# Two taps of the shifted k in one VectorE product, and dy written over the gradient's rows

## The chip, the cores and the metric

One core of a Trainium2 chip. The metric is device time in microseconds (us). The profile follows one execution; its times are from the start of that execution's span. PE is the matmul engine (PEld its weight loads), DVE the vector engine, ACT the scalar engine, POOL GpSimd, and SP the engine that issues most of the DMAs. Every engine works through its own instructions in a fixed order and waits at semaphores for the others.

## The reference, cut to what matters

The kernel computes a layer's output and its gradients. With S = 2048 positions, D = 512 channels:

```
xn      = layernorm(q)
k_shift = sum over t = 0..3 of k[s - t] * shift_k[:, t]        # per channel, bf16
kv      = k_shift * v
y       = causal long convolution of kv with ssm_k (by FFT)  + kv * ssm_D
out     = q + xn * y + (xn W_gate * xn W_up) W_down
gradients of out with respect to q, k, v, shift_k, ssm_k, ssm_D, W_gate, W_up, W_down
```

The gradient that enters is `grad_out` (go). The convolution's backward pass starts from dy = go * xn, which must go through the same transform as kv and as ssm_k.

## The kernel before, in words

Position s = 16 p + r lies on partition p, row r. The rows are handled as eight blocks b of two rows, so that a block of q, k, v or go is a tile of 128 x 2 x 512 bf16 (256 KB). There are three stretches.

*The front* (to about 120 us). The DVE normalizes each block (`norm`, L315 to L345: statistics, a root on ACT at L331, a reciprocal, the rows, then a store of xn to `XN` in DRAM). `kernel_spec` (L407) turns ssm_k around and sends its sixteen rows through the first transform matmul, `stage1` (L360); the results in PSUM are evicted to `fst` by DVE and ACT in turn, and `wgu_transposes` (L442) turns the two up-projections around. `pre(b)` (L376) makes for a block dy = go * xn (L381), the four-tap sum `ks` from `kh` (L389, L391, L392), stores `ks` to `KS` in DRAM (L397), multiplies it by v (L399), and sends dy and kv through `stage1`. `kh` is k with three boundary rows ahead of its sixteen; it is loaded by four DMAs (`load_k`, L308): rows 0 to 2 by two, rows 3 to 10 and rows 11 to 18 by one each. `skb` holds the taps on all partitions.

*The feed-forward part.* `ffn1(ch)` and `yb(ch)` (L495, L537) run the gated layer for chunks ch of 256 positions. They fill `hd`, which is stored to `HDD` in DRAM, and `bx`, which is stored to `BX`. Work of the front and of the spectral groups (`groups`, L737) is the side generator, and the loop at L883 takes some steps of it after each step of the main one.

*The rest* (from about 300 us): inverse transforms, weight gradients, and the final elementwise work. The change does not touch it.

What sets the order: each call emits instructions, and a scheduler then places them on each engine's queue; up to the end of `tables(3)` (L699) the program fixes the relative order of those engines' instructions by `manual_schedule`, but a later instruction whose inputs are there can still be put between them. The tile framework adds the waits. It also takes care of memory: the pool `st1` (L675) is laid over that of the tables' temporaries and can be written only when those are done. In `st1` lie `kh`, `dy_b`, `t_b` and the turned ssm_k tiles `kn`, one buffer each of `dy_b` and `t_b`. The tiles of q and go (`x_b`, `go_b`, L298 and L304) lie in another pool, with four and three buffers. So the load of block b + 4 of q, and of block b + 3 of go, must wait until the earlier block's last reader is done. PSUM tiles of two banks (`pf`, `pgu`, `ptk`, `pw`) share three buffers (L252), so a matmul group waits for the eviction of the group three before it. SP issues loads and stores in one queue. Each DMA signals one of eight semaphores in turn, so an issue also waits for the landing of the DMA eight issues before it.

Of the kernel before, what the change touches and what calls it, by code (L numbers as in the profile page):

```python
# [8 lines left out]
BF = mybir.dt.bfloat16  # L9
F32 = mybir.dt.float32  # L10
I32 = mybir.dt.int32
ALU = mybir.AluOpType
# [6 lines left out]
D = 512  # L19
F = 1376  # L20
R = 16
P = 128
# [168 lines left out]
def kernel(  # L191
# [24 lines left out]
    nc = tc.nc  # L216
# [45 lines left out]
    skb = const.tile([P, 4, D], BF, name="skb")  # L262
# [97 lines left out]
    def stage1(sig, src, i, r, evac):  # L360

        if r % 2 == 0:
            FST[sig] = stp.tile([P, 2, 2, D], BF, name="fst", bufs=4)
        st = FST[sig]
        pf = P2("pf", [P, 2, D])
        for c in range(2):
            point = sig == 0 and r == 0
            nc.tensor.matmul(pf[:, c, :], lhsT=TB.W1[:, c, :], rhs=src[:, i, :], start=True, stop=not point)  # L368
            if point:

                nc.tensor.matmul(pf[:, c, :], lhsT=TB.W1[0:1, c, :], rhs=Drow, start=False, stop=True)
        evac(st[:, :, r % 2, :], pf[:])
        if r % 2 == 1:
            nc.sync.dma_start(FD[sig, :, :, r - 1:r + 1, :], st[:])

    def pre(b):  # L376

        xn, go = XG.pop(b)
        v = VB.pop(b)
        dy = ST["st1"].tile([P, 2, D], BF, name="dy_b")  # L380
        nc.vector.tensor_tensor(dy[:], go[:], xn[:], op=ALU.mult)  # L381
        yield
        ks = stp.tile([P, 2, D], BF, name="ks_b")
        t = ST["st1"].tile([P, 2, D], BF, name="t_b")
        for n, j in enumerate((3, 2, 1, 0)):
            src = ST["kh"][:, 2 * b + 3 - j:2 * b + 5 - j, :]
            w = skb[:, j:j + 1, :].to_broadcast((P, 2, D))
            if n == 0:
                nc.vector.tensor_tensor(ks[:], src, w, op=ALU.mult)  # L389
            else:  # L390
                nc.vector.tensor_tensor(t[:], src, w, op=ALU.mult)  # L391
                nc.vector.tensor_tensor(ks[:], ks[:], t[:], op=ALU.add)  # L392
            if n == 1:
                stage1(2, dy, 0, 2 * b, act)
                stage1(2, dy, 1, 2 * b + 1, act)
                yield
        nc.sync.dma_start(KS[:, 2 * b:2 * b + 2, :], ks[:])  # L397
        kv = v
        nc.vector.tensor_tensor(kv[:], ks[:], v[:], op=ALU.mult)  # L399
        yield  # L400

        def last():
            stage1(1, kv, 0, 2 * b, act)
            stage1(1, kv, 1, 2 * b + 1, act)
        LATE.append(last)
# [265 lines left out]
    ST = {}  # L671
# [40 lines left out]
    def front():  # L712
        for b in range(8):
            if b == 0:
                late_loads()
                with tc.issue_after(TB.last.ins):
                    norm(2)
            elif b < 6:
                norm(b + 2)
            if LATE:  # L720
                LATE.pop(0)()
            yield
            if b == 0:
                yield from kernel_spec()
                yield from wgu_transposes()
                WTS.append(True)
            if 0 < b < 7:
                load_v(b + 1)
            yield from pre(b)
            if b < 5:  # L730
                load_x(b + 3)
        LATE.pop(0)()
        yield
# [470 lines left out]
```

## Time and profile before

| | us |
|---|---|
| median of 3 runs | 488.27 |
| all runs | 490.54, 488.27, 486.96 |
| the profiled execution | 485.82 |
| its span, first to last instruction | 484.1 |
| PE busy in the span | 470.3 |
| DVE busy | 340.6 |
| ACT busy | 318.2 |
| DVE, the 24 products L391 | 16.5 |
| DVE, the 24 additions L392 | 16.5 |
| DVE, the 8 products L389 | 5.5 |
| DVE, the 8 products L381 | 5.4 |

The profiled execution took 485.82 us, 1.7 more than its span. Durations are of single instructions; consecutive DVE instructions overlap by some 0.07 to 0.09 us, so an instruction of 0.69 us holds the queue for about 0.60.

### The profile page before, as it was taken

To read this page: it belongs to the slowest core of one execution; us is meant where nothing else is said; L and a number is where in the kernel's file an instruction comes from. 1 tells how busy PE (TensorE), PEld (TensorE's weight loads), DVE (VectorE), ACT (ScalarE), POOL (GpSimd) and SP (SyncE) were. 2 spreads that over 40 slices of the span, in tenths; PEclk is the share of its full clock that TensorE was granted. 3 is DMA by queue.
4 is the path that set the end of the run, shared out by engine and by line. 5 is a ranking of instruction groups with operands and counts; after the bars stand their busy time and mean duration, and the time that the engine had idled before them with its cause. 6 is when DMAs were issued, how large, how long until landed. Compare 5 with 4: busy or idle time off the path is not lost.

```text
span 484.1 us, 10517 instructions
## 1 busy us (share of the span) xinstructions
PE 470.3 (97%) x4335; PEld 313.7 (65%) x4335; DVE 340.6 (70%) x622; ACT 318.2 (66%) x354; POOL 15.3 (3%) x31
## 2 busy tenths in 40 slices
PE   7998999999999999999999999999999999999977
PEld 6866754647638547447447744567777788777775
DVE  7889969988274768667686865013276899999780
ACT  4976896759658678779779974466577524543141
POOL 8010000000000000000000000020000000000000
PEclk9999999999999999999999999999999999999999
DMA  8999998999997965978968298999999979699747
GB/s 269 374 379 359 294 263 313 349 308 338 310 303 277 252 220 196 295 251 254 301 214 258 78 334 294 399 327 307 321 396 384 367 263 404 203 254 245 209 149 246
DMA packets 105469, 139.87 MB, mean 289 GB/s; under 512 B 33323, under 2 KB 78800, under 8 KB 103758
## 3 DMA queue, kind: packets, MB, share of 16 engines
q1 hardware_dynamic: 103838, 137.84, 86.1%
q10 hardware_dynamic: 1584, 1.36, 1.0%
q8 instruction: 34, 0.56, 0.5%
q14 instruction: 13, 0.11, 0.1%
HBM read 68.45 MB, written 63.41 MB: 272 GB/s over the span
## 4 chain that ended last, share of the span: by engine, by line
PE 61%; DVE 21%; DMA 13%; issue 2%; ACT 2%; SPq 0%; DVEq 0%; ACTq 0%
PE px L553 16%; PE pgu L510 13%; PE py L546 8%; PE pdh L516 6%; PE pu L1038 5%; DMA out_dram<-o 4%; PE pf L368 3%; PE pg L611 3%; PE ps L582 3%; PE pd L1002 2%; DMA HDD<-hd 2%; DVE dxn L1126 2%; DVE tk L1093 2%; DVE dxn L1120 2%; DVE e L1121 2%
## 5 line engine op out<-in xcount | busy, mean ns | idle before, releaser
L553 PE MATMUL px<-WT,hd 128*128 128x512 bf16 (+1 forms) x352 | 81.0, 380 | 0.0
L1038 PEld LDWEIGHTS <-xnC 128*128 128x128 bf16 x704 | 67.1, 98 | 8.8 <-issue 0.9
L553 PEld LDWEIGHTS <-hd 128*128 128x128 bf16 (+1 forms) x352 | 32.8, 98 | 44.4 <-issue 7.5
L1038 PE MATMUL pu<-natd,xnC 128*128 128x256 bf16 x512 | 58.5, 273 | 0.2 <-ACT nath L235 0.2
L235 ACT CAST GO<-pg 128x1024 bf16<-128x1024 f32 x48 | 46.3, 1017 | 12.8 <-PE pg L611 6.6
L235 ACT CAST SP<-ps 128x1024 bf16<-128x1024 f32 x48 | 46.6, 1029 | 11.9 <-PE ps L582 10.9
L510 PE MATMUL pgu<-xt,Wu 128*128 128x256 bf16 (+1 forms) x352 | 53.2, 273 | 0.6 <-DVE fst L238 0.4
L235 ACT CAST gu<-pgu 128x1024 bf16<-128x1024 f32 (+1 forms) x48 | 45.4, 947 | 12.3 <-PE pgu L510 11.9
L510 PE MATMUL pgu<-xt,Wg 128*128 128x256 bf16 (+1 forms) x352 | 52.8, 273 | 0.2 <-DMA Wg<-in_B_w_gate_dram 0.2
L598 DVE TENSOR_TENSOR T<-SP 128x2048 bf16<-128x2048 bf16 x24 | 29.4, 1223 | 30.8 <-ACT SP L235 30.8
L516 PE MATMUL pdh<-gt,WdT 128*128 128x256 bf16 (+1 forms) x352 | 47.1, 273 | 0.1
L510 PEld LDWEIGHTS <-Wu 128*128 128x128 bf16 (+1 forms) x352 | 32.9, 100 | 14.7 <-issue 10.2
L546 PE MATMUL py<-Wd,hd 128*128 128x512 bf16 (+1 forms) x176 | 41.4, 380 | 0.0
L235 ACT CAST og<-pu 128x1024 bf16<-128x1024 f32 (+1 forms) x11 | 10.9, 994 | 46.2 <-PE pu L1038 25.6
L235 ACT CAST fst<-pf 128x1024 bf16<-128x1024 f32 x40 | 39.1, 1034 | 0.8 <-ACT dh L235 0.5
L235 ACT COPY natd<-pt 128x2048 bf16<-128x2048 bf16 x16 | 30.0, 1876 | 13.5 <-PE pt L846 13.5
L516 PEld LDWEIGHTS <-WdT 128*128 128x128 bf16 (+1 forms) x352 | 34.9, 100 | 5.2 <-issue 0.2
L510 PEld LDWEIGHTS <-Wg 128*128 128x128 bf16 (+1 forms) x352 | 34.8, 100 | 4.1 <-DMA Wg<-in_B_w_gate_dram 0.5
L530 DVE TENSOR_TENSOR hd<-gu 128x512 bf16<-128x512 bf16 (+1 forms) x48 | 19.1, 398 | 19.0 <-ACT gu L235 19.0
L531 DVE TENSOR_TENSOR hd<-gu,dh 128x1024 bf16<-128x1024 bf16 (+1 forms) x48 | 30.8, 642 | 1.0
L1002 PE MATMUL pd<-goC,nath 128*128 128x512 bf16 x128 | 30.1, 379 | 0.0
L546 PEld LDWEIGHTS <-hd 128*128 128x128 bf16 (+1 forms) x176 | 16.4, 98 | 20.7 <-issue 3.3
(171 smaller groups left out, 698.0 us busy)
## 6 DMA issues: line engine op xcount, KB each, us to landing
HDD<-hd SPq DMA_DIRECT2D x35, 384.0 KB, 3.6
FD<-fst SPq DMA_DIRECT2D x24, 512.0 KB, 4.5
X<-FD SPq DMA_DIRECT2D x24, 512.0 KB, 4.7
GD<-GO SPq DMA_DIRECT2D x24, 512.0 KB, 3.9
g<-GD SPq DMA_DIRECT2D x12, 1024.0 KB, 7.9
hb<-HDD SPq DMA_DIRECT2D x8, 1344.0 KB, 8.5
bb<-BX SPq DMA_DIRECT2D x8, 512.0 KB, 6.9
BX<-bx SPq DMA_DIRECT2D x7, 512.0 KB, 3.6
```

The source lines that it names most:

```text
L235: nc.scalar.copy(o, i)
L368: nc.tensor.matmul(pf[:, c, :], lhsT=TB.W1[:, c, :], rhs=src[:, i, :], start=True, stop=not point)
L510: nc.tensor.matmul(pgu[:w, i, t, :], lhsT=W[:, c, f0:f0 + w], rhs=xt[:, :, c, :], start=(c == 0), stop=(c == NC4 - 1))
L516: nc.tensor.matmul(pdh[:w, i, :], lhsT=WdT[:, c, f0:f0 + w], rhs=gt[:, :, c, :], start=(c == 0), stop=(c == NC4 - 1))
L530: nc.vector.tensor_tensor(hd[:fw, fb0:fb0 + n, 0, :], gu[:fw, :n, 0, :], gu[:fw, :n, 1, :], op=ALU.mult)
L531: nc.vector.tensor_tensor(hd[:fw, fb0:fb0 + n, 1:3, :], gu[:fw, :n], dh[:fw, :n].unsqueeze(2).to_broadcast((fw, n, 2, 256)), op=ALU.mult)
L546: nc.tensor.matmul(py[:], lhsT=hd[:fw, fb, 0, ss], rhs=Wd[:fw, fb, :], start=(fb == 0), stop=(fb == NFB - 1))
L553: nc.tensor.matmul(px[:], lhsT=hd[:fw, fb, t, ss], rhs=W[:fw, fb, :], start=(t == 1 and fb == 0), stop=(t == 2 and fb == NFB - 1))
L582: nc.tensor.matmul(ps[32 * q:32 * q + 32, a, :], lhsT=TB.EF[64 * a:64 * a + 64, 4 * g + q, ri].rearrange("p k j -> p (k j)"), rhs=X[64 * a ...
L598: tt(W[:].rearrange("p c a d -> p c (a d)"), A[:, i:i + 1].rearrange("p c a d -> p c (a d)").to_broadcast((P, 2, 2 * D)), B[:].rearrange(" ...
L1002: nc.tensor.matmul(pd[:fw, :], lhsT=nat_h(fb, r), rhs=goC[:, r, :], start=(r == 0), stop=(r == R - 1))
L1038: nc.tensor.matmul(pu[:, c, :, :fw], lhsT=xnC[:, r, cs(c)], rhs=nat_d(fb, r), start=(r == 0), stop=(r == R - 1))
```

## The change

Two edits in `pre(b)`. dy no longer has a tile of its own: it is written over the block's go tile. And the four taps are taken two at a time: one product of 128 x 2048 elements (two taps, two rows, 512 channels) reads three rows of `kh`, the middle one twice, and the taps' rows in falling order; its result `t` has twice the size. Each pair of taps is then added up in `ks`. So a block has two products and three additions in place of four products and three additions.

```
-        dy = ST["st1"].tile([P, 2, D], BF, name="dy_b")
+        dy = go
         nc.vector.tensor_tensor(dy[:], go[:], xn[:], op=ALU.mult)
         yield
         ks = stp.tile([P, 2, D], BF, name="ks_b")
-        t = ST["st1"].tile([P, 2, D], BF, name="t_b")
-        for n, j in enumerate((3, 2, 1, 0)):
-            src = ST["kh"][:, 2 * b + 3 - j:2 * b + 5 - j, :]
-            w = skb[:, j:j + 1, :].to_broadcast((P, 2, D))
-            if n == 0:
-                nc.vector.tensor_tensor(ks[:], src, w, op=ALU.mult)
+        t = ST["st1"].tile([P, 2, 2, D], BF, name="t_b")
+        for n in (0, 2):
+            s = ST["kh"][:, 2 * b + n:2 * b + n + 3, :]
+            part, row, elem = s.ap
+            src = bass.AP(s.tensor, s.offset, [part, [row[0], 2], [row[0], 2], elem])
+            w = skb[:, 2 - n:4 - n, :]
+            part, row, elem = w.ap
+            w = bass.AP(w.tensor, w.offset + row[0], [part, [-row[0], 2], [0, 2], elem])
+            nc.vector.tensor_tensor(t[:], src, w, op=ALU.mult)
+            nc.vector.tensor_tensor(ks[:], t[:, 0] if n == 0 else ks[:], t[:, 0 if n else 1], op=ALU.add)
+            if n:
+                nc.vector.tensor_tensor(ks[:], ks[:], t[:, 1], op=ALU.add)
             else:
-                nc.vector.tensor_tensor(t[:], src, w, op=ALU.mult)
-                nc.vector.tensor_tensor(ks[:], ks[:], t[:], op=ALU.add)
-            if n == 1:
                 stage1(2, dy, 0, 2 * b, act)
                 stage1(2, dy, 1, 2 * b + 1, act)
                 yield
```

In the additions, the pair n = 0 writes `ks = t[0] + t[1]`; the pair n = 2 adds `t[0]` and then `t[1]`.

Nothing else in the source differs. The scheduler puts the changed program's instructions in another order, though, on DVE, ACT and SP, between the start and some 120 us; on PE six matmuls (three `pdh`) come earlier and the rest keeps its order, and POOL's order is the same. After 130 us all the orders agree. The lines behind L397 have numbers larger by 3 in the changed kernel.

## The prediction

> **What bounds the kernel now.** I read the page first, then busy time by stretches, then the waits, then the queues one by one.
>
> ```profile
> PE 470.3 (97%) x4335; PEld 313.7 (65%) x4335; DVE 340.6 (70%) x622; ACT 318.2 (66%) x354; POOL 15.3 (3%) x31
> PE   7998999999999999999999999999999999999977
> DVE  7889969988274768667686865013276899999780
> ```
>
> PE is nearly full everywhere, so a change in the front is worth what it adds to or takes from PE's waits there. The table by stretches (PE, PEld, DVE, ACT, POOL, then clock, DMA share, GB/s) and the waits of PE up to 170 us show where these are:
>
> ```profile
> 24.00:36.00 12.00, 11.31 (x98) 8.14 (x96) 10.74 (x24) 8.80 (x12) 1.37 (x1) 1.00 1.07 382
> 36.00:48.00 12.00, 10.18 (x87) 7.73 (x86) 11.20 (x20) 8.45 (x10) 0.00 (x0) 1.00 0.96 362
> 48.00:60.00 12.00, 11.60 (x107) 8.82 (x105) 11.90 (x20) 9.98 (x13) 0.00 (x0) 1.00 0.91 288
> ...
> PE ptk L413 <- DVE fst L238: 1.5, 1, 1.5
> ...
> PE pf L368 <- ACT fst L235: 0.9, 1, 0.9
> ```
>
> From 36 to 60 us the DVE has no idle time left, and PE waits for its evictions (fst): 1.48 at 41.97, and again at 57.87. The 0.9 is at 77.99. From 84 to 120 PE shows no wait. The DVE, in turn, starts that stretch by waiting for k, and k waits its turn on SP. DVE's timeline, then SP's:
>
> ```profile
> 32.30 1.18 DVE L238 CAST fst<-pf 128x1024 bf16<-128x1024 f32 x1
> ...
> 36.76 0.69 DVE L389 TENSOR_TENSOR ks_b<-kh,skb 128x1024 bf16<-128x1024 bf16 x1 [1.99 <-DMA kh<-in_A_k_dram]
> ...
> 40.70 1.22 DVE L238 CAST fst<-pf 128x1024 bf16<-128x1024 f32 x1
> ```
>
> ```profile
> 25.45 1.56 SPq L348 DMA_DIRECT2D XN<-x_b  x2
> 27.06 0.45 SPq L300 DMA_DIRECT2D x_b<-in_A_q_dram  x1
> 27.77 1.20 SPq L534 DMA_DIRECT2D HDD<-hd  x2
> 29.57 0.34 SPq L310 DMA_DIRECT2D kh<-in_A_k_dram  x1
> 30.42 0.37 SPq L311 DMA_DIRECT2D kh<-in_A_k_dram  x1
> ```
>
> The reader sees k's boundary rows issued at 29.57 and 30.42 and used at 36.76, while the DMA share is about 1: transfers land in turn, some 6.3 us after their issue.
>
> **The change part by part.** *Cheaper products.* The groups by form give the price:
>
> ```profile
> L598 DVE TENSOR_TENSOR T<-SP 128x2048 bf16<-128x2048 bf16 x24 | 29.4, 1223 | 30.8 <-ACT SP L235 30.8
> L391 DVE TENSOR_TENSOR t_b<-kh,skb 128x1024 bf16<-128x1024 bf16 x24 | 16.5, 686 | 0.2
> ```
>
> Two products of 0.687 become one of 1.22: 0.15 saved, 16 times, 2.4 us of DVE by 118 us. Four such pairs lie in the full stretch 36 to 60 (0.6 us); the others lie where PE does not wait for the DVE. L391 and L598 each read a row of one operand twice and still add 1024 elements for 0.53 us. No row of the trace reads an operand's rows in falling order. Its bounds are 1.22 and about 2.3 us (with float32 operands 256 elements take 0.42 in L1067 and 512 take 0.69 in L548, 1.04 ns an element, so 2048 take 2.3); I take 1.22, from the row of the same shape and type. The Trainium skill ("VectorE: DVE Perf Modes", What auto-detection actually checks) asks of the faster mode that tensors be 16-bit with step one along the elements, which by that rule leaves 1.22 standing; no run so far shows a falling row.
>
> *dy without st1.* dy's tile no longer waits for the tables' memory, so the order puts dy(0) right behind the first rows, ahead of the copy of xt at 8.44 (idle 0.49 before it), and dy(1) between the masks at 22.75 and 22.93. The first costs 0.1, which the 0.64 us of idle time at 12.72 covers. The second pushes what follows on DVE by 0.60; it takes 0.60 out at 31.09, where dy(0) stood.
>
> *SP, the step that costs most.* With dy(0) and dy(1) done early, two loads of q, blocks 4 and 5, come free and are put on SP ahead of k: XN(0), XN(1), x3, **x4**, HDD, **x5**, HDD, k. But x4 goes into block 0's buffer, which the store XN(0) still reads. That store is issued at 25.45 and lands 6.3 later, at 31.8. So SP, which stood free at 27.5, stands until 31.8; behind it wait two HDD stores, x5 (XN(1) lands at 32.4) and all of k. At 0.5 us each (35.19 to 35.72 in SP's timeline), k's boundary rows are issued at 33.8 and 34.3 in place of 29.57 and 30.42. When do they land? From below: 34.3 plus 3.1, the landing time of the FD store at 57.88, is 37.4. From above, in turn: x4 at 31.8 + 3.2 (v at 79.1) = 35.0, HDD 1.0, x5 0.66, HDD 1.0 (spacings of the landings at 32.4 to 35.1), k 1.65 (35.1 to 36.76): 39.3. I take K = 38.8, nearer the upper end because DMA share is 1 there: 2.0 later.
>
> *DVE and ACT behind it.* In the new order the statistics of x3 stand ahead of the first fst; x3 lands at 33.1 (27.06 + 6.0), so that fst runs at 35.4, not 32.30. PE's second group of stage one and the ACT wait for it, but k is later still. Then ACT has the root of x3 ahead of the eviction of gu(1), and that root needs an aggregate that the DVE makes only behind the first wide product. Counted from K: product 1.15, aggregates 0.25, root 0.2, gu 1.0: at K + 2.6 PE gets its buffer; pf 0.43, pdh 0.22; the next pgu needs the second fst, at K + 3.25 (1.15 + 0.2 + 0.62 + 0.1 + 1.15), and takes 1.75, pdh 0.22, pf 0.43: the transposes that waited at 41.97 start at K + 5.75. Before it was 36.76 + 5.21. So PE is later by 2.0 + 0.54 = 2.6 at this point. The rest of the stretch up to the fst at 56.60, summed the same way (four products at 1.15, seven more operations at 0.60 to 0.65, two more statistics at 0.60, the same evictions), ends 21.75 behind K, before 21.06: 2.6 or 2.7 again, with 0.7 us of slack at each PE wait between. The 0.6 us of cheaper products are in this sum; the two statistics, drawn forward because x4 is there early, eat them.
>
> *58 to 84.* The evictions of the turned weights on ACT (59.45) and PE behind them shift as they are. A new wait: go(3) now reuses the tile that PE's dy(0) matmuls read until 68.5, before only DVE's dy. So go(3) is issued at 71.2 (before 61.73), lands 3.4 later (go at 70.07), and DVE stands at dy(3) for it, with the aggregate of x6 behind: dy 0.6, reciprocals 0.25, sum 0.6, rows 1.3, product 1.15, aggregates 0.2; ACT's root waits for that with fst of dy(1) behind it, 1.3: PE at 77.55 plus the shift. Before, PE stood at 77.99. So 0.45 is won back: 2.15 is left. v's load, also freed by PE, was so before. The root of x7 comes next: from 78.8 the DVE has two wide products, ten operations of 0.6 and two statistics up to x7's aggregate, about 9.4, so root and gu(2) end on ACT at 89.5; PE wants that buffer at 87.31 + 2.15 = 89.5: nothing more, and nothing to spare. Later dy and kv are made 2 to 9 us before PE takes them, and go(4) to go(7), issued when PE's dy three blocks before is done, land over 10 us before theirs is due.
>
> **Sum.** 2.0 (k later) + 0.54 (order) - 0.45 (won back) = +2.1 us. The profiled execution is 485.82 (span 484.1 and 1.7 around it), so 487.9; it lies 2.4 under the median of the runs shown, 488.27, and against that the forecast is 490.4.
>
> **The rivals.** *Hidden:* k is not late. If the engines are empty enough for K = 37.4 or less, or if the loads land as before, +0.5 to +1.1 is left of the order and 0.45 to 0.9 comes back at 77.99: +0.2, 488.5. For it: SP's pause empties the DMA queue. Against: five transfers of 1.66 MB then come in a bunch.
>
> *Faster:* every saved 0.15 counts, because DVE is full from 36 to 60 and 9 to 10 tenths until 118: -2.4 us, 485.9. It decides if K stays at 36.8 and PE's wait at 77.99 (0.9) goes. Against it: beyond 84 us PE has no wait. The Trainium skill ("VectorE: DVE Perf Modes", Rules for kernel authors) says to minimize the count of DVE operations; by that rule the 16 fewer would show.
>
> *The go ring:* go(3) or go(4) lands after 6.3 us, as in the crowd at 25, not 3.4. Then ACT's root at 79 is 2.9 later and PE stands for it: 493.3. For it: three blocks of go now hang on PE, and SP stands at each.
>
> *Falling rows at half speed:* 16 x 1.1 us more DVE. Four lie in the full stretch: 4.3, less 0.7 slack; the other twelve overrun the idle DVE of 60 to 118 by about 3: +9 in all, 497.5.
>
> **How the numbers follow.** Forecast 0.58, hidden 0.17, faster 0.08, go ring 0.11, half speed 0.06. The range: K from 37.4 to 39.3 and an error of 1 us in the sums give +0.2 to +3.8, so 488.5 to 492.1; the three runs shown lie 3.6 apart, half of which I add on both sides: 486.7 to 493.9. That reaches the go ring and most of the hidden case, and leaves out half speed and most of the faster one. A measurement tells about 1% from no change, 4.9 us. Faster by over 1%: 0.03, a third of the faster case; slower: all of half speed, half of the go ring, a little of the forecast: 0.14; within 1%: 0.83.
>
> **What would show it.** Right: SP's k issues at 33.5 to 34.5 with x4 at 31.8 ahead; the first wide product at 38 to 39.5 with DVE idle before it; wide products of 1.22 us; the transposes L413 (now L416) at 44 to 45; DVE waiting for go(3) near 74. Wrong: k's product at 37 or before, or products of 2 us, or PE waits between 84 and 120, or another time in the rest, which I take as unchanged.

## The result, and the profile after

The changed kernel took 493.46 us (median of six runs, 491.06 to 494.09); the kernel before, run beside it, 487.72 (six runs). The ratio is 1.0101, with a 95% interval of 1.0068 to 1.0134. The profiled execution took 494.09, with a span of 491.9.

Where the time went is read by setting each matmul of the one trace against the same matmul of the other. PE's order is nearly the same, so the difference of the start times is how far PE is behind at that point:

| before, us | changed is later by |
|---|---|
| to 29 | 0.0 |
| 31.8 | 1.15 |
| 34.4 | 0.55 |
| 35.3 to 36.1 | 1.18 |
| 42.0 (the transposes L413) | 6.19 |
| 44 to 56 | 6.20 |
| 58 to 76 | 5.94 |
| 84 to 382 | 5.86 |
| 394 to 459 | 10.19 |
| 471 to the end | 7.85 |

Nearly all of the change's own loss arises between 36 and 42 us. It stays at 5.86 for 300 us, and the difference of the medians is about the same, 5.74. The other 2 us of the profiled pair come in the tail, where PE waits for a load from DRAM (2.8 at 393 for `hb` in the changed kernel, with 3.4 us at half the clock behind it; 2.7 for `g` near 460 in the one before); the queues agree there, and PE's place at the end against that at 300 us varies from -1.3 to +1.9 among the kernels below, so nothing is read from it.

The page's lines (busy sums; PE and DVE busy and the granted clock in 40 slices of 12.3 us), then the table by stretches (PE, PEld, DVE, ACT, POOL, clock, DMA share, GB/s):

```profile
PE 471.3 (96%) x4293; PEld 317.2 (64%) x4335; DVE 338.7 (69%) x606; ACT 317.9 (65%) x354; POOL 15.7 (3%) x31
...
PE   8986999999999999999999999999999799999997
...
DVE  7885999968356668676777865013266799999880
...
PEclk9997999999999999999999999999999989999999
```

```profile
24.00:36.00 12.00, 10.62 (x94) 7.89 (x93) 10.24 (x26) 8.86 (x11) 1.37 (x1) 1.00 0.86 310
36.00:48.00 12.00, 7.06 (x30) 4.18 (x31) 6.76 (x11) 2.91 (x4) 0.00 (x0) 0.72 1.01 369
48.00:60.00 12.00, 11.62 (x107) 9.42 (x108) 11.65 (x17) 10.74 (x12) 0.00 (x0) 0.99 0.82 253
```

The 16 DVE operations are gone (622 to 606) and DVE's busy time is 1.9 less. But in 36 to 48, where DVE was busy for 11.2 of 12 us, it is now busy for 6.8, PE for 7.1, and PE's clock was granted at 0.72. A stretch that was full now stands half empty, and is slow where it isn't. PE's waits up to 170 us, then ACT's timeline and DVE's there:

```profile
PE pf L368 <- ACT gu L235: 4.4, 1, 4.4
...
PE pf L368 <- ACT fst L235: 0.8, 1, 0.8
```

```profile
41.01 0.29 ACT L331 ACTIVATE rstd<-mv,eps_t 128x2 f32<-128x2 f32 x1 [5.13 <-DVE mv L325]
41.21 0.99 ACT L235 CAST gu<-pgu 128x1024 bf16<-128x1024 f32 x1
```

```profile
35.19 1.21 DVE L238 CAST fst<-pf 128x1024 bf16<-128x1024 f32 x1
39.59 1.23 DVE L392 TENSOR_TENSOR t_b<-kh,skb 128x2048 bf16<-128x2048 bf16 x1 [3.19 <-DMA kh<-in_A_k_dram]
```

Read from below: DVE stands 3.19 for k, to 39.59 (before 36.76). x3's aggregates are behind that product, ACT's root waits for them (5.13), the eviction of gu is behind the root, and PE waits for its buffer (4.4). On SP:

```profile
27.20 4.76 SPq L300 DMA_DIRECT2D x_b<-in_A_q_dram  x2
32.06 0.39 SPq L537 DMA_DIRECT2D HDD<-hd  x1
32.55 0.41 SPq L300 DMA_DIRECT2D x_b<-in_A_q_dram  x1
33.05 0.60 SPq L537 DMA_DIRECT2D HDD<-hd  x1
33.75 0.52 SPq L310 DMA_DIRECT2D kh<-in_A_k_dram  x1
34.33 0.76 SPq L311 DMA_DIRECT2D kh<-in_A_k_dram  x1
```

x4 is the second issue of the first line, at 31.62, when the store XN(0) had landed (31.57); then HDD, x5, HDD, k. Last, PE's timeline behind the wait:

```profile
42.26 1.01 PE L368 MATMUL pf<-kn,W 128*128 128x512 bf16 x2 [4.45 <-ACT gu L235]
...
43.49 1.06 PE L513 MATMUL pgu<-xt,Wu 128*128 128x256 bf16 x4
44.34 1.06 PE L513 MATMUL pgu<-xt,Wg 128*128 128x256 bf16 x4
...
48.16 1.16 PE L416 MATMUL ptk<-ident,ssk 128*128 128x128 bf16 x16 [0.20 <-issue]
```

Four matmuls of 256 columns take 0.85 from start to start here, and 0.44 elsewhere. The granted clock is 0.5 from 41.3 to 48.1: it fell inside the wait, 3.5 us after its start at 37.8, and came back just ahead of the transposes.

### The profile page after: what moved, and what is told of

Read it like the earlier page. It is cut to its first block, busy times and chain, and to the rows that moved or that the text cites. A ratio compares the mean times of both kernels' runs of the same rounds, so it can differ in the third digit from the quotient of the medians.

```text
span 491.9 us, 10468 instructions
## 1 busy us (share of the span) xinstructions
PE 471.3 (96%) x4293; PEld 317.2 (64%) x4335; DVE 338.7 (69%) x606; ACT 317.9 (65%) x354; POOL 15.7 (3%) x31
## 4 chain that ended last, share of the span: by engine, by line
PE 61%; DVE 17%; DMA 15%; ACT 3%; issue 2%; SPq 0%; ACTq 0%; DVEq 0%
PE px L556 14%; PE pgu L513 13%; PE py L549 7%; PE pdh L519 6%; PE pu L1041 5%; DMA out_dram<-o 4%; DMA Wg<-in_B_w_gate_dram 4%; PE pg L614 3%; PE ps L585 3%; PE pd L1005 2%; PE pf L368 2%; DMA hb<-HDD 2%; DMA out_dram<-e 2%; PE pt L849 2%; DVE tk L1096 1%
## 5 line engine op out<-in xcount | busy, mean ns | idle before, releaser
L556 PE MATMUL px<-WT,hd 128*128 128x512 bf16 (+1 forms) x338 | 78.3, 379 | 1.8 <-issue 1.6
L549 PE MATMUL py<-Wd,hd 128*128 128x512 bf16 (+1 forms) x169 | 40.3, 380 | 0.6 <-issue 0.3
L601 DVE TENSOR_TENSOR U<-SP 128x2048 bf16<-128x2048 bf16 x24 | 29.3, 1219 | 0.0
```

Of the source, the lines that this page charges most:

```text
L549: nc.tensor.matmul(py[:], lhsT=hd[:fw, fb, 0, ss], rhs=Wd[:fw, fb, :], start=(fb == 0), stop=(fb == NFB - 1))
L556: nc.tensor.matmul(px[:], lhsT=hd[:fw, fb, t, ss], rhs=W[:fw, fb, :], start=(t == 1 and fb == 0), stop=(t == 2 and fb == NFB - 1))
L601: tt(W[:].rearrange("p c a d -> p c (a d)"), A[:, i:i + 1].rearrange("p c a d -> p c (a d)").to_broadcast((P, 2, 2 * D)), B[:].rearrange(" ...
```

## The experiments

*Theory*, from this trace: the loss comes from dy over go. It makes dy(0) and dy(1) early, x4 and x5 get ahead of k on SP, k lands 2.8 later, PE stands 4.45 us, and the low clock behind that costs more. *Rivals:* the wide products and their order; the root of x3 ahead of gu on ACT; that the low clock costs nothing, since the evictions set the pace.

Two numbers are read from each trace: K, when the first product with k starts, and T, when the transposes start that before were at 41.97. "PE" is how far PE is behind the kernel before at 84, and at 300 us.

| kernel | K | T | T - K | PE, 84 / 300 | median | ratio to before, 95% |
|---|---|---|---|---|---|---|
| before | 36.76 | 41.97 | 5.21 | | 487.72 | |
| changed | 39.59 | 48.16 | 8.57 | 5.86 / 5.86 | 493.46 | 1.0101 (1.0068 to 1.0134) |
| e2_dy_only | 39.59 | 47.45 | 7.86 | 4.53 / 10.50 | 496.33 | 1.0146 (1.0119 to 1.0172) |
| e3_dy_late | 36.66 | 41.79 | 5.13 | -1.12 / -0.44 | 486.91 | 0.9976 (0.9952 to 1.0000) |
| e4_k_first | 36.81 | 42.51 | 5.70 | 0.06 / 0.06 | 486.28 | 0.9976 (0.9949 to 1.0004) |
| e5_pe_kept_busy | 39.96 | 45.89 | 5.93 | 5.19 / 5.70 | 493.73 | 1.0095 (1.0072 to 1.0119) |
| e5b_pe_kept_busy | 40.18 | 45.88 | 5.70 | 4.33 / 4.32 | 492.01 | 1.0083 (1.0057 to 1.0108) |
| e6_root_behind_gu | 40.86 | 48.65 | 7.79 | 10.54 / 10.53 | 495.59 | 1.0141 (1.0101 to 1.0181) |
| e7_k_first_root_behind | 36.66 | 42.20 | 5.54 | -0.63 / 4.86 | 492.41 | 1.0078 (1.0045 to 1.0111) |
| e8_k_before_x3 | 36.12 | 41.70 | 5.58 | -0.83 / 1.38 | 487.71 | 1.0001 (0.9972 to 1.0031) |
| e9_v7_before_x | 36.77 | 42.31 | 5.54 | -0.52 / 0.85 | 489.36 | 1.0027 (0.9997 to 1.0056) |
| e10_k_held_alone | 39.81 | 44.95 | 5.14 | 3.05 / 4.11 | 491.72 | 1.0062 (1.0038 to 1.0087) |
| e11_dy_only_v7 | 39.72 | 45.32 | 5.60 | 2.97 / 4.22 | 494.68 | 1.0127 (1.0087 to 1.0167) |
| e12_k_before_xn | 35.53 | 40.68 | 5.15 | -2.24 / -1.34 | 486.19 | 0.9981 (0.9951 to 1.0012) |

The median of before beside them was 488.19 (e2 to e5), 487.52 (e5b to e11) and 488.14 (e12). K, T and PE are of one profiled execution each, and its time can lie some 3 us from the median (e5b: 489.21, the fastest of its eleven); the medians and ratios are of 6 to 12. Places such as "at 78" or "near 121" are times of the kernel before, against which PE is compared.

### One half alone: dy over go, narrow products

```
-        dy = ST["st1"].tile([P, 2, D], BF, name="dy_b")
+        dy = go
```

(on the kernel before). The other half alone was not run: with its own tile for dy and the wide `t_b`, `st1` would need 33 KB of each partition, against 31 in both kernels. The next run stands for it.

> Only dy is written over go; the products stay narrow, as before. Theory (dy over go makes dy(0) and dy(1) early, x4 and x5 come free and go on SP ahead of k): k issued at 33.5 to 34.5, its first product near 39.6, as in the changed kernel. In this order the root of x3 stands behind the eviction of gu on ACT, so PE does not stand for gu but, from 38.8, for the fst of the DVE at K + 3.25 = 42.9; if that wait of 4 us lowers the clock as in the changed kernel, the transposes L413 start at 47 to 47.5 (+5), else at 45.4 (+3.5). Time 3.5 to 5.5 over before, 491 to 493. Rival (the loss comes from the wide products and their order): transposes at 42.0 and a time within 1 us of before.

K is 39.59 as in the changed kernel, to the hundredth, and T 47.45: the theory's numbers. The loss is there without a wide product, and the first rival falls. The time was missed, by 3 to 5 us: PE lost another 4.7 near 121, in a wait for kv(7) of 3.2, of which more below.

### The whole change with dy(0) and dy(1) late

```
-        nc.vector.tensor_tensor(dy[:], go[:], xn[:], op=ALU.mult)
+        if b < 2:
+            with tc.issue_after(TB.last.ins):
+                nc.vector.tensor_tensor(dy[:], go[:], xn[:], op=ALU.mult)
+        else:
+            nc.vector.tensor_tensor(dy[:], go[:], xn[:], op=ALU.mult)
```

> The whole change, but dy(0) and dy(1) are held behind the last instruction of the tables, about where they stood before. Theory: x4 and x5 stay behind k on SP, k issued at 29.6, first wide product at 36.8, transposes at 41.7 to 42.3, clock 1.00 throughout; time as before, between 1.0 less and 0.5 more: 486.7 to 488.2. Rival (wide products): PE later by over 2 us at the transposes, time 490 or more. Rival (go ring): a DVE wait for go near 70 to 80 and PE later behind it by over 2 us.

All of it came as the theory said: k issued at 29.38, K 36.66, T 41.79, clock 1.00. Holding two DVE operations back takes the whole loss away. DVE does stand for go(3), 1.71 to 73.89, where the prediction put it, but PE does not wait behind it: its wait of 0.9 at 77.99 is gone. With wide products, then, PE is 0.18 earlier at T, and 0.83 more is won at 78. That second part can't be put down to the wide products: e2, whose products are narrow, wins 0.84 there as well.

### The whole change with k ahead of x4 and x5

```
             if b < 5:
-                load_x(b + 3)
+                if b in (1, 2):
+                    with tc.issue_after(LK["k"].ins):
+                        load_x(b + 3)
+                else:
+                    load_x(b + 3)
```

(`LK["k"]` is the last of k's four loads).

> The whole change, dy(0) and dy(1) early, but the loads of x4 and x5 (and of their go) held behind the four loads of k on SP. The root of x3 still stands ahead of the eviction of gu on ACT. Theory: k issued at 29.6, first wide product at 36.8, aggregates to 38.0, root, gu done at 39.4; PE waits 1.6 there, no fall of the clock, transposes at 42.3 to 42.7; time 0.3 to 1.0 over before: 488.0 to 488.7. Rival (the order on ACT and DVE alone costs the 5.9): transposes at 45 or later, time 492 or more.

PE waits 0.81 for gu, and then, in its timeline:

```profile
42.51 1.17 PE L418 MATMUL ptk<-ident,ssk 128*128 128x128 bf16 x16
```

dy is early and the root of x3 still stands ahead of gu, and the loss is gone: only k's place on SP is changed. T - K is 5.70, the prediction's 5.75 for this order. The time, 486.28, lies 1.7 under the expected.

### PE kept busy in the gap

```
+            mm = nc.tensor.matmul(pf[:, c, :], lhsT=TB.W1[:, c, :], rhs=src[:, i, :], start=True, stop=not point)
+            if sig == 0 and r == 3 and c == 1:
...
+                for _ in range(16):
+                    WIDE.append(nc.tensor.matmul(pf[:, c, 0:8], ...).ins)
...
```

The same product is written sixteen times more. The repeats are entered eight columns wide, so that the scheduler moves little, and widened to 512 once the order stands.

> The whole change, with one matmul of 512 columns (row 3 of the turned ssm_k) repeated sixteen times in the gap where PE waits 4.45 us for gu; the result is the same, and the order on the engines is that of the changed kernel but for a few pdh. Theory (the low clock is a cost of its own, 2.8 us): the wait shrinks to 1.4, four matmuls of 256 columns take 0.44 and not 0.86 from start to start, transposes at 45.3 to 45.7 in place of 48.16, and all behind is 2.5 to 2.8 earlier than in the changed kernel: 490.7 to 491.0. Rival (the late k and the evictions set the pace, the clock only fills the wait): transposes at 47.5 or later, time 493 to 494.

T is 45.89, 0.2 above the theory's range; the time is the rival's. From 44 to 76 PE was 1.8 to 2.0 better than in the changed kernel, and lost 1.0 of it at 78: the scheduler had put x6's load behind two transposing loads on SP, DVE stood for it to 76.22, and ACT's root and PE behind that. So it was done once more, with fourteen of the sixteen repeats put in after the order was fixed:

> As the run in which PE was kept busy, but the sixteen repeated matmuls are put in after the order of the queues is fixed, so that SP, ACT and PE have the order of the changed kernel and DVE but for two swaps of neighbours. In the first form the load of x6 went on SP behind two transposing loads, and PE lost 1.0 at 78 of the 2.0 to 2.3 that it had gained. Theory (the low clock costs some 2 us of its own): transposes at 45.3 to 45.9, PE 3.4 to 4.0 behind the kernel before from 42 to 76, and 3.4 to 4.2 behind it from 84 on; time 491.0 to 492.0. Rival (the evictions and loads behind take the gain back whatever the order): 5 or more behind from 84 on, time 493 to 494.

```profile
37.77 3.62 PE L373 MATMUL pf<-kn,W 128*128 128x512 bf16 x15
...
42.84 0.59 PE L369 MATMUL pf<-kn,W 128*128 128x512 bf16 x2 [1.12 <-ACT gu L236]
...
43.49 0.60 PE L518 MATMUL pgu<-xt,Wu 128*128 128x256 bf16 x4
43.92 0.60 PE L518 MATMUL pgu<-xt,Wg 128*128 128x256 bf16 x4
...
45.88 1.17 PE L421 MATMUL ptk<-ident,ssk 128*128 128x128 bf16 x16
```

Here K came 0.59 later than in the changed kernel (k's boundary rows landed at 40.1), and T still 2.28 earlier: with the clock kept up, T - K is 5.70, against 8.57. The low clock's price is 2.87 at the transposes. PE's place came 0.1 to 0.2 us outside what was expected (3.9 to 4.2 behind up to 76, 4.33 from 84 on): 1.5 better than the changed kernel, with the later K in it. The median is 1.5 lower, but the intervals of the two ratios overlap, so the clock's price rests on T and on PE's place. There the third rival falls.

### The root behind gu

```
+        if root and b == 3:
+            with tc.issue_after(GU[1, 0].ins):
+                norm_std(b)
```

(on the changed kernel; `GU[1, 0]` is the eviction of gu; x4's statistics are held behind an `fst` in the same way).

> The whole change with dy(0) and dy(1) early and k late as in it, but ACT's root of x3 held behind the eviction of gu (and x4's statistics held behind an fst on DVE, so that nothing else moves). Theory (the late k is the cause, the root's place little): first wide product near 39.6, PE no longer waits for gu but from 38.8 for the fst at K + 3.25 = 42.9, the clock falls again, transposes at 47.2 to 47.7, 5.3 to 5.7 later than before; time 492.5 to 493.5. Rival (the root ahead of gu is the main cause): transposes at 45 or earlier, time under 491.

PE no longer waits for gu, and waits 4.47 for the fst behind K instead; the clock falls, and T - K is 7.79. The root's place costs little: the second rival falls too. The time was missed: K came 1.3 later still, and at 78 PE lost another 3.6 (a wait of 2.8 for an fst on ACT).

### Both, and a place on SP at the other end

> Both: x4 and x5 behind k on SP, and the root of x3 behind gu on ACT; dy(0) and dy(1) early, wide products. Theory: k's product at 36.8, no wait for gu, transposes at 41.7 to 42.2, PE level with or up to 1.0 ahead of the kernel before from 84 on; time 486.0 to 487.5, level with the run with k first. Rival (early dy costs on its own): 488.5 or more.

Up to 118 this went as expected, and PE was 0.63 ahead; the time, 492.41, was missed by 5 us. Then DVE, and PE behind it, stood for v(7):

```profile
122.64 0.69 DVE L407 TENSOR_TENSOR v_b<-ks_b,v_b 128x1024 bf16<-128x1024 bf16 x1 [9.71 <-DMA v_b<-in_A_v_dram]
```

```profile
111.25 0.61 SPq L581 DMA_DIRECT2D X<-FD  x1
...
113.91 1.08 SPq L357 DMA_DIRECT2D v_b<-in_A_v_dram  x1
```

The load of X (512 KB) takes 6.9 us from its issue to its landing, and v(7), issued behind it, 8.6. In e4 v(7) was issued at 109.82, ahead of X, and had landed by 114.8. In e2, whose loss near 121 was as large, v(7) stood behind X too. Both were run again with `g_load` under `tc.issue_after(LV[7].ins)`; only the order on SP between the two changes: v(7) goes ahead of X and of one store.

> As the run with k first and the root behind gu, in which PE stood 4.0 us near 120 for kv(7), because the load of v(7) stood on SP behind the first load X from FD. Here that load of X (and those after it) is held behind v(7); nothing else moves. Theory (4.85 us lost there come from that place on SP alone): no wait of PE for v_b, PE 0.6 ahead of the kernel before from 84 to 130; time 486.0 to 487.5 and under that of before by up to 1. Rival (the X load, later now, is waited for instead): a wait of 1 us or more for X near 130, time 488 or more.

The wait for v is gone and PE is 0.52 ahead from 84 to 130; then it stands 1.3 for X, the rival's wait, and the median of 489.36 is the rival's too. That leaves PE 0.85 behind, 3 us of median better than e7, but not better than e4.

> The run with dy over go alone (narrow products), with the load X from FD held behind the load of v(7). In the first form PE lost 4.7 us near 121 behind that. Theory (a place on SP again, not the narrow products): no wait for v_b there, PE 5.8 behind the kernel before from 88 on, as in the changed kernel; time 493.0 to 494.0. Rival (narrow products make kv late): a wait for v_b or ks of 2 us or more stays, time 495 or more.

Again no wait for v_b. But the profile is not the one expected: PE is 3.9 behind from 88, not 5.8, and the median of 494.68 lies between the two expectations. The queues up to 110 us are those of e2. PE's timelines, e2 and then e11:

```profile
42.81 1.01 PE L510 MATMUL pgu<-xt,Wu 128*128 128x256 bf16 x4 [4.19 <-DVE fst L238]
```

```profile
35.61 1.06 PE L511 MATMUL pgu<-xt,Wu 128*128 128x256 bf16 x4
...
42.93 0.60 PE L511 MATMUL pgu<-xt,Wu 128*128 128x256 bf16 x4 [2.32 <-DVE fst L238]
```

In this execution the clock fell earlier, from 34.4 to 37.8, where PE had time to lose; the gap behind was 2.3 and the clock held. T - K is 5.60, against 7.86 in e2 with the same K within 0.13. One execution can differ from another by 2 us in this way, which may be why the median lies between.

### x3 behind k as well

The edit is e7's, with x3's load held behind k too.

> As the last, and x3's load is put behind k as well. If k is what the stretch waits for, k issued by 28.9, first product at 35.8 to 36.3, PE 0.5 to 1.0 earlier than in the last run at the transposes; time 485.5 to 486.5. Rival (x3 late in turn: its rows, stores and the chunk's transposing loads come later): PE later again between 50 and 80, time 487.5 or more.

K and T came as in the theory's part (36.12, T 0.5 earlier than in e7), and so did a time in the rival's range (487.71), though not where the rival had put it: PE stood 1.65 for `bx` near 100 and gave back 1.8 there, and it is 1.4 behind at 300. No gain.

### A late k by itself

```
+        held = nc.sync.dma_start(HOLD[:], XN[0:1, 0, 0:64])
+        with tc.issue_after(held.ins):
+            nc.sync.dma_start(ST["kh"][1:113, 0:3, :], k_n[0:112, R - 3:R, :])
...
```

(on e3; `HOLD` is 128 bytes in DRAM).

> The run with dy(0) and dy(1) held late (whose queues are nearly those of before), with one more DMA of 128 bytes on SP ahead of two HDD stores and of k, which reads XN(0) from DRAM and so makes SP stand until that store has landed, near 31.6. Nothing else on any queue differs. It tells the price of a late k by itself. Theory: k's boundary rows issued at 33.0 to 33.8, first product at 38.2 to 39.0 (x4 and x5 are not ahead of it), transposes 5.1 to 5.2 behind that, 43.3 to 44.2, if the clock holds, PE then 1.5 to 2.4 later than in the run without the extra DMA; time 488.3 to 489.3. If PE's gap of some 3.5 us lowers the clock, up to 2.5 more, behind the transposes. Rival (a late k costs nothing without the other order): time as without, 486 to 487.

DVE's timeline and PE's:

```profile
39.81 1.23 DVE L399 TENSOR_TENSOR t_b<-kh,skb 128x2048 bf16<-128x2048 bf16 x1 [5.05 <-DMA kh<-in_A_k_dram]
```

```profile
42.88 0.59 PE L371 MATMUL pf<-kn,W 128*128 128x512 bf16 x2 [3.05 <-DVE fst L238]
44.95 1.86 PE L423 MATMUL ptk<-ident,ssk 128*128 128x128 bf16 x16 [1.48 <-DVE fst L238]
```

One tiny DMA that makes SP stand for the landing of XN(0) brings back most of the loss: K 3.15 later, T 5.14 behind K as expected, and behind the two waits the clock is down (sixteen transposes take 1.86, not 1.16), for 1.2 more. PE is 4.4 behind e3 at 44, and 4.55 at 300; the ratios, 1.0062 and 0.9976, say 4.2 us. K itself was expected at 38.2 to 39.0 and came at 39.81, with k's rows issued at 33.42 and 33.99: issued 0.3 earlier than in the changed kernel and used 0.2 later, without x4 and x5 ahead. So the standing of SP alone makes k as late, and the transfers of x4 and x5 aren't needed for it; why k came no earlier with less ahead of it is open.

### k ahead of the stores of xn

The other way round, from e3: `store_xn(0)` and `store_xn(1)` moved behind `load_k()`.

> The run with dy(0) and dy(1) held late, and the stores XN(0) and XN(1) put on SP behind k's four loads, not ahead of them. If k's landing is set by what is in the DMA queues ahead of it, 512 KB fewer there let k land earlier: first product at 34.9 to 35.8 in place of 36.66 (DVE is free for it at 34.75), transposes 5.1 behind, at 40.1 to 40.9, PE 1.0 to 1.7 earlier than in the run without this; time 485.0 to 486.5, under both kernels. Rival (k lands some 6 us behind its issue whatever is ahead): product at 36.3 or later, time 487 or more. Behind 60 us the queues differ a little from that run's, which may take some of it.

K 35.53, T 40.68, PE 1.1 ahead of e3 there: as expected. k was issued only 0.4 to 0.7 earlier than in e3 and landed 1.1 earlier. At 300 us PE is 1.34 ahead of before and 7.2 ahead of the changed kernel. The median, 486.19, is as expected too, but the interval takes in 1: e3, e4 and e12 all lie under both kernels, clearly under the changed one, and none is told from the one before.

## Why the prediction was right or wrong

The forecast was +2.1, the median difference is 5.74. It named the place, the cause and the sign, but the sum lacks a term. That the range, 486.7 to 493.9, held the median of 493.46 is in part luck. Without the scatter added on both sides it ended at 492.1, and a lower clock was in none of its terms. The kernel before also came out 0.55 lower beside the changed one than in the three runs from which the forecast starts: the difference, 5.74, is above the +5.6 of the range's upper end. The 1% that the prediction took as what can be told was just passed (1.01%); it had given a chance of 0.14 to that. Of its signs, the issues on SP, the width of the products and the wait for go(3) came (at 78.6, not near 74); the first wide product, at 39.59, is 0.09 over the stated 39.5, and the transposes missed 44 to 45 by 3 us.

*Right.* dy(0) and dy(1) early (8.03 and 22.96), x4 and x5 ahead of k, SP standing to 31.6, k's rows issued at 33.75 and 34.33 (forecast 33.8 and 34.3). The wide product takes 1.21 to 1.23, in falling rows as well, so the rival of half speed falls. By the Trainium skill ("VectorE: DVE Perf Modes", What auto-detection actually checks) the type and the step along the elements decide the faster mode; these rows agree. The order behind K costs 0.49: e4 and e5b have T - K of 5.70, before 5.21. The forecast was 5.75, though its terms (3.25 + 1.75 + 0.22 + 0.43) add up to 5.65. The go ring costs PE far less than its rival had: DVE stands for go(3) 0.57 in the changed kernel and 1.71 in e3, and no PE wait lies between 84 and 120.

*Too small: K.* Forecast 38.8 with 39.3 as the upper bound, measured 39.59: +2.83 in place of +2.0. The bound from above took the transfers in turn and was nearly exact: x4 landed at 34.83 (35.0 there), HDD at 35.82 (36.0). The step that failed is the choice of a value under it. The argument that SP's pause empties the DMA queues does not bear it out: in e10 a pause alone leaves k at 39.81.

*Missing: the clock.* This is the step that failed most. The forecast counted PE's wait for gu, up to K + 2.6 = 41.4, as a shift, with every matmul behind it at its usual length. PE's clock fell in that wait (0.5 from 41.3 to 48.1). That is 2.87 us at the transposes, by T - K of 8.57 against 5.70 in e5b, and 2.83 + 0.49 + 2.87 makes the 6.19 measured there. The Trainium skill ("TensorE: Matmul & The Clock Gate", What's actually happening) states that an idle window of about 3.4 us takes PE's clock to half, and about as long a busy time brings it back. From 37.8, where the wait starts in the trace, to the forecast's 41.4 is 3.6. (The last section shows that shorter waits were followed by a low clock too.)

*Not won back: the 0.45 at 77.99.* The changed kernel keeps 0.83 of that wait (0.90 before), 0.07 won. The chain is the one that the prediction named; from DVE's, ACT's and PE's timelines:

```profile
78.63 0.69 DVE L381 TENSOR_TENSOR go_b<-go_b,x_b 128x1024 bf16<-128x1024 bf16 x1 [0.57 <-DMA go_b<-in_grad_out_dram]
...
82.61 0.29 ACT L331 ACTIVATE rstd<-mv,eps_t 128x2 f32<-128x2 f32 x1 [1.88 <-DVE mv L325]
...
83.85 0.59 PE L368 MATMUL pf<-v_b,W 128*128 128x512 bf16 x2 [0.83 <-ACT fst L235]
```

DVE stands for go(3); x6's second aggregate is behind dy(3), its rows and a wide product; ACT's root waits for that aggregate, and PE for the fst behind the root. From dy(3) to PE it takes 5.22 (4.1 + 1.3 in the forecast). What came later is go(3): it was issued at 74.62, since PE, which frees its tile, was 5.9 behind there and not 2.6, and it took 3.9 us, not 3.4, to land. PE has lost the wait in e3, e4 and e7, where k is on time, but also in e2 and e10, where it is late; in e3, e4, e7 and e10 x6's aggregates stand ahead of dy(3) on DVE. So the order on DVE and go(3)'s landing set this wait by the trace; no run changed one of them alone.

*The rivals.* "Hidden" needed K at 37.4 or before; it was 39.59. "Faster" needed PE to wait for the DVE: with k on time and wide products (e3) PE is 1.1 earlier at 84, most of it the wait at 78 that e2 loses with narrow products too, and 0.4 is left at 300 us; the ratio's interval ends at 1.0000. The saved DVE time is real (1.9 us of busy time) and hardly on the path. So the rule that the prediction cited for this rival, fewer DVE operations (the Trainium skill, "VectorE: DVE Perf Modes", Rules for kernel authors), pays here only where an engine waits for the DVE.

## What to carry to other kernels

When an edit frees a buffer or drops a wait, look at what becomes ready early and where it lands on a queue that works in order: a load that must wait for a store to land holds up every load behind it, and the one that the stretch hangs on should go first. Price a PE wait of nearly 3 us or more as the wait and a slow stretch behind it, which cost 1.2 (e10) to 2.9 us (changed) more here, and look for what keeps PE busy or splits the gap. When an experiment moves one thing, compare the queues further on as well: e2, e5, e7 and e9 were decided by a load's place 35 to 90 us behind the edit.

## What the runs showed of the hardware

PE's low clock. Behind the first 30 us, all eight waits of PE of 2.8 us or more had a granted clock of 0.5 in them or close behind: 4.45 and, at 393, 2.82 (changed), 4.19 and 3.23 (e2), 4.47 and 2.85 (e6), 4.01 (e7, near 120) and 3.05 with 1.48 close behind it (e10). Matmuls took about twice as long there. Of eleven waits between 2.1 and 2.7 three were followed by it (2.55 in e10, 2.24 in e5 and 2.10 in e12, all in the tail) and eight were not, the longest being 2.69 in the kernel before. Each of these low stretches lasts 3.41 us, or 6.83 behind the waits of 4.45, 4.19 and 4.47, and the stretches at full clock are whole multiples of 3.41 too (27.31 in e4, 81.92 in e2, 344.75 in the changed kernel). So the clock seems to be set at steps of 3.41 us, and where in a step a short wait falls may decide; no run tests that. The length agrees with the window of the Trainium skill cited above. The rule that PE must be idle for that long does not: waits of 2.1 to 3.2 us were enough here.

Beside that, in e4, e5, e6, e8, e9 and e11 the clock was also low for 3.41 us, from a point between 32.5 and 34.4, after a wait of only 1.1 at 31 that is followed by matmuls with one row of weights and by transposes; in the changed kernel, e2, e5b and e7 it was not, with the same instructions. What decides that is open.

A load's landing. The last of k's boundary rows (45 KB, on fifteen partitions) took 5.0 to 6.1 us from issue to landing in the runs where they were issued at 34 to 35, with a DMA share of about 1, and a load of 256 KB behind the 512 KB of X took 8.6 (e7).
